# Moving half of one weight load to another queue, and cutting one VectorE task into six, in an attention and feed-forward kernel with a written-out order

## The chip, the cores and the metric

The kernel runs on one core of one Trainium2 chip. The core has a matrix engine (TensorE, PE in the profile; its weight loads are PEld), VectorE (DVE), ScalarE (ACT), GpSimd (POOL) and SyncE (SP), which issues most DMAs. Matmuls write to PSUM, eight banks of 128 partitions by 512 float32; all other data lie in SBUF. Each engine works through its own instruction stream in order and waits on semaphores for what other engines or DMAs have to deliver. The metric is the device time of one execution in microseconds (us), the median of several; lower is better.

## The reference

The input x has 2048 rows of 512 bfloat16 numbers. Three things are computed from it and mixed:

```python
g = sigmoid((x * gate_w).sum(-1, keepdims=True))     # one number per row
a = attention(x, wq, wk, wv, wo, beta)
b = ((relu(x @ W_gate) * (x @ W_up)) @ W_down)       # inner width 1792
out = g * a + (1 - g) * b
```

The attention has 32 heads of width 16. The rows are cut into 4 segments of 512. Inside a segment it is a causal softmax attention. Beside it each head keeps a memory, `M += phi(k).T @ v` and `z += sum(phi(k))` with `phi(t) = t + 1 if t > 0 else exp(t)`, from which the next segments read `phi(q) @ M / (phi(q) @ z)`. A gate per head, `sigmoid(beta)`, weighs memory against softmax. The head gates, called so below, are these 32 numbers and one minus them, spread over the partitions in the layouts that later steps want.

## The kernel before

All weights are loaded once and stay in SBUF. The work goes by segment (four) and inside a segment by column chunk c of 128, which holds 8 heads. For each segment x is wanted transposed (`xT`) and, for the row gate, untransposed (`xn`). `proj_q`, `proj_k` and `proj_v` are matmuls with the weights, each followed by a copy out of PSUM (VectorE, or ScalarE for half of v). For k, three masked copies into `KT` (L569) follow the copy. Scores come in fills of four PSUM banks (L617, and L630 for the diagonal blocks); ScalarE takes their exp (L639), GpSimd masks them (L668), and TensorE multiplies them with v (L690). `memory` (L801) forms M and z. `ffn_tasks` (L845) forms relu(gate) on ScalarE (L854) and its product with up on VectorE (`hT`, L860). `out_tile` (L871) adds the down projection and the attention's output projection in one PSUM bank.

Nearly every step of this is a task: `plan.add(engine, duration, key, emit, deps, ...)`. Durations, latencies and the table `LANDS` (when each first load is thought to be in) are numbers of a planner that ran beforehand. It is not in the file; its results are: `ORDER` lists all tasks by number in the order in which they are emitted, and `UNITS` gives for each buffer that a task needs (a PSUM bank, a ring buffer) which one it gets. Each engine executes its tasks in the order of that list. So the durations in the file have no effect on the chip; the order does.

What comes ahead of the list, in the order of the program: the loads (L300 to L328), each on the queue of the engine that issues it. SyncE (`nc.sync`) issues nearly all; ScalarE (`nc.scalar`) issues half of segment 0's `xn` and one quarter of `wq`. Segment 0's x comes in two halves: columns 0 to 255 as rows in `xn`, which TensorE transposes by a matmul with the identity (L500), and columns 256 to 511 by a DMA transpose (L304). So q of segment 0 is formed in two halves (L540 to L545): the first half of its four matmuls per chunk needs the first half of wq and `xn`, the second half needs wq's second half (L306) and the DMA transpose.

Two more pieces matter. `heat` (L901) is a warm-up: seven matmuls on constants in front of everything. `head_gates` (L385) is one VectorE task of 25 small instructions; it waits for `eb` (L398, ScalarE's exp of beta), which waits for the load of `betab` (L312). The row gate's dot product with `gate_w` is L417, one VectorE task per 128 rows; it reads `xn`, which is loaded anew for each segment (L276).

Of the kernel before, what the change touches and what calls it, by code (L numbers as in the profile page):

```python
# [178 lines left out]
def kernel(  # L179
# [205 lines left out]
    def head_gates():  # L385
# [4 lines left out]
        for m in range(4):  # L390
            rows = slice(32 * m, 32 * m + 32)
            nc.vector.tensor_copy(gcat[rows, 1], g[rows, 1, :, m])  # L392
            for c in range(NC):
                nc.vector.tensor_copy(gcat[rows, 0, c], g[rows, 0, c, (m + c) % 4])  # L394
# [11 lines left out]
    def K(unit, part=0.0):  # L406
        return unit * UNIT + part
# [563 lines left out]
```

## Time and profile before

| | us |
|---|---|
| median of 3 runs | 264.85 (264.78 to 265.1) |
| the profiled execution's own time | 264.56 |
| its span in the profile | 262.6 |
| TensorE busy | 258.0 (98%) |
| VectorE busy | 203.6 (78%) |
| ScalarE busy | 183.2 (70%) |
| GpSimd busy | 63.2 (24%) |

The span is the time from the first to the last instruction of the core; the rest of the execution's time lies around it. A matmul's row in the profile lasts longer than the distance to the next one, as matmuls overlap, so waits of TensorE are best read from the distances between starts. In a timeline line the columns are start, length, engine, line, operation, what is written and read, the shape and how many; in brackets stands how long the engine was idle before it and what it waited for. In the lines of waits the figures are the total in us, how often, and the longest.

### The profile page before, as it was taken

What the parts mean: (1) busy time and instruction counts of PE and PEld (TensorE: products, weight loads), DVE (VectorE), ACT (ScalarE), POOL (GpSimd) and SP (SyncE); (2) the same over time, 40 slices, a digit from 0 to 9 for tenths busy, and PEclk for the clock granted to TensorE, in tenths of its full rate; (3) what the DMA queues carried; (4) which work ended last, traced back from release to release, by engine and by line L of the source; (5) the groups of instructions that cost most, each with busy time, mean ns of one, the idle gap of its engine ahead of it and who ended that gap; (6) DMA issues with size and microseconds to landing.
All of it is one profiled execution on the core that took longest, in us unless ns stands there. A gap on an engine that the chain in (4) does not pass through costs nothing.

```text
span 262.6 us, 8919 instructions
## 1 busy us (share of the span) xinstructions
PE 258.0 (98%) x3867; PEld 117.4 (45%) x3867; DVE 203.6 (78%) x472; ACT 183.2 (70%) x168; POOL 63.2 (24%) x168
## 2 busy tenths in 40 slices
PE   8999999999999999999999999999999999999995
PEld 3434434454444354544444444444445444445454
DVE  2799999999895756959998977584998786768622
ACT  3299889999788688888586767788575767883000
POOL 8024353212321323232111321122121242121000
PEclk9999999999999999999999999999999999999999
DMA  7999974020402122100211112002110101120011
GB/s 193 301 264 308 312 148 122 4 42 12 94 3 74 46 67 67 49 2 2 81 21 25 54 31 103 22 12 82 35 47 6 54 2 62 70 76 19 2 42 42
DMA packets 31566, 19.72 MB, mean 75 GB/s; under 512 B 16040, under 2 KB 29992, under 8 KB 31528
## 3 DMA queue, kind: packets, MB, share of 16 engines
q1 hardware_dynamic: 31112, 18.90, 26.0%
q8 instruction: 30, 0.49, 0.8%
q10 hardware_dynamic: 416, 0.26, 0.3%
q14 instruction: 8, 0.07, 0.1%
HBM read 13.21 MB, written 2.55 MB: 60 GB/s over the span
## 4 chain that ended last, share of the span: by engine, by line
PE 91%; DMA 3%; SPq 2%; DVE 2%; issue 0%; ACT 0%
PE ps L463 52%; PE ps L467 21%; PE ps L617 8%; PE ps L690 7%; DMA betab<-in_A_beta_dram 3%; SPq L266 2%; PE ps L630 1%; PE ps L810 1%; DVE gcat L394 1%; SPq L304 1%; PE ps L746 0%; PE ps L786 0%; SPq L310 0%; DVE gcat L392 0%; DVE hT L860 0%
## 5 line engine op out<-in xcount | busy, mean ns | idle before, releaser
L639 ACT ACTIVATE E<-ps 128x2048 bf16<-128x2048 f32 x64 | 120.1, 1876 | 30.0 <-PE ps L617 20.1
L668 POOL TENSOR_SCALAR_AFFINE_SELECT E<-E 128x256 bf16<-128x256 bf16 x128 | 54.6, 451 | 172.9 <-ACT E L639 172.8
L860 DVE TENSOR_TENSOR hT<-ps,rgr 128x512 bf16<-128x512 f32 x56 | 38.0, 685 | 20.3 <-PE ps L463 11.8
L463 PE MATMUL ps<-xT,wu_sb 128*128 128x512 bf16 x172 | 47.1, 380 | 0.0
L854 ACT ACTIVATE rgr<-ps 128x512 bf16<-128x512 f32 x56 | 32.7, 596 | 16.9 <-PE ps L463 10.3
L463 PE MATMUL ps<-xT,wg_sb 128*128 128x512 bf16 x152 | 41.9, 380 | 0.5 <-DVE hT L860 0.5
L463 PE MATMUL ps<-wd_sb,hT 128*128 128x512 bf16 (+1 forms) x165 | 38.3, 353 | 0.0
L721 DVE STREAM_TRANSPOSE T<-ps 128x512 f32<-128x512 f32 x32 | 22.4, 706 | 7.5 <-PE ps L690 7.2
L617 PE MATMUL ps<-QT,KT 32*128 32x320 bf16 (+3 forms) x512 | 25.4, 273 | 0.0
L463 PEld LDWEIGHTS <-wu_sb 128*128 128x128 bf16 x172 | 15.6, 98 | 19.3 <-issue 2.5
L463 PEld LDWEIGHTS <-wg_sb 128*128 128x128 bf16 x152 | 14.1, 98 | 18.1 <-issue 2.5
L886 DVE TENSOR_SCALAR osr<-ps,ngcol 128x512 bf16<-128x512 f32 (+2 forms) x18 | 12.4, 689 | 11.8 <-PE ps L467 8.0
L463 PEld LDWEIGHTS <-hT 128*128 128x128 bf16 x165 | 14.2, 98 | 16.1 <-issue 2.5
L467 PE MATMUL ps<-wd_sb,hT 128*32 128x512 bf16 (+1 forms) x348 | 21.3, 362 | 0.0
L467 PE MATMUL ps<-xT,wg_sb 128*32 128x512 bf16 x288 | 19.8, 379 | 0.0
L617 PEld LDWEIGHTS <-KT 32*128 32x128 bf16 x512 | 7.6, 92 | 26.4 <-issue 25.4
L690 PE MATMUL ps<-E,Vp 128*17 128x320 bf16 (+3 forms) x512 | 19.3, 273 | 0.0
L639 ACT ACTIVATE Em<-ps 128x2048 bf16<-128x2048 f32 x8 | 15.0, 1873 | 3.1 <-PE ps L630 3.1
L463 PE MATMUL ps<-wv_sb,xT 128*128 128x512 bf16 x60 | 16.4, 380 | 0.0
L463 PE MATMUL ps<-xT,wq_sb 128*128 128x512 bf16 x54 | 15.4, 385 | 0.3 <-DMA wq_sb<-in_A_wq_dram 0.3
L467 PE MATMUL ps<-xT,wu_sb 128*32 128x512 bf16 x208 | 14.9, 379 | 0.0
L463 PE MATMUL ps<-xT,wk_sb 128*128 128x512 bf16 x54 | 14.6, 380 | 0.0
(102 smaller groups left out, 299.7 us busy)
## 6 DMA issues: line engine op xcount, KB each, us to landing
out_dram<-osr SPq DMA_DIRECT2D x15, 128.0 KB
wd_sb<-in_B_W_down_dram SPq DMA_DIRECT2D x2, 896.0 KB
xn<-in_A_x_dram SPq DMA_DIRECT2D x3, 512.0 KB
cdr<-coefs SPq DMA_DIRECT2D x6, 256.0 KB
xn<-coefs SPq DMA_DIRECT2D x6, 256.0 KB
wg_sb<-in_B_W_gate_dram SPq DMA_DIRECT2D x2, 512.0 KB
wu_sb<-in_B_W_up_dram SPq DMA_DIRECT2D x2, 512.0 KB
wg_sb<-in_B_W_gate_dram SPq DMA_DIRECT2D x2, 384.0 KB
```

The costliest lines, as they stand in the source:

```text
L266: eng.dma_start(out=dst, in_=src)
L304: nc.sync.dma_start_transpose(out=xT[0][:, NC // 2:NC, :], in_=x[0:L, halves[1]])
L463: nc.tensor.matmul(out, lhsT=lhsT, rhs=rhs, start=start, stop=stop)
L467: nc.tensor.matmul(out[r], lhsT=lhsT[:, r], rhs=rhs, start=start, stop=stop, tile_position=(0, 32 * j))
L617: nc.tensor.matmul(ps[:, j * L + o:j * L + o + L - q], lhsT=KT[i][rows, kb, 3 * r:3 * r + 2].rearrange("p h q -> p (h q)"), rhs=QT[i][rows ...
L639: last_exp[0] = [plan.add("ACT", 66 + 4 * L / 1.2, key, lambda: nc.scalar.activation(dst, ps[:, 0:4 * L], ACT.Exp, scale=SCALE), [a] + war ...
L668: nc.gpsimd.affine_select(out=m[:, :, o:o + HP], in_=m[:, :, o:o + HP], compare_op=ALU.is_ge, fill=0.0, base=HP, pattern=[[0, 4], [1, HP]] ...
L690: nc.tensor.matmul(bank(sl)[32 * m:32 * m + HW, q:q + w], lhsT=(Vp[i] if n < 4 else Vm)[:, kb, r, 4 * c + j, 0:HW], rhs=rhs, start=(n == 0 ...
L721: done.append(plan.add("DVE", 633, key - RL, lambda r=r, sl=sl: nc.vector.transpose(T[ts.i][:, r], bank(sl)), [a] + done, 75 if r else 0, ...
L854: r = plan.add("ACT", 478, key - RL, lambda sl=gsl, rs=rs: nc.scalar.activation(rgr[rs.i][:], bank(sl), ACT.Relu), [g], ACL, frees=[gsl])
L860: nc.vector.tensor_tensor(hT[hs1.i][:], bank(sl), rgr[rs.i][:], ALU.mult)),
L886: nc.vector.tensor_scalar(osr[os.i][:, n0 - c0:n1 - c0], bank(sl)[:, 0:n1 - n0], ngcol[:, tt:tt + 1], None, ALU.mult)),
```

## The change

It has four parts, and a new `ORDER` and `UNITS` that go with them.

- wq's second half is loaded from ScalarE's queue instead of SyncE's. It is issued as ScalarE's third DMA, right behind its share of the first half, while SyncE issues the DMA transpose of x.
- The task `head_gates` becomes six tasks: the three instructions that form the gates, four times `row_gates(m)` (five copies each), and `pair_gates` (two instructions). Their durations add up to 3240 ns in place of 2000. The instructions are the same 25.
- The last matmul of the warm-up has 128 columns instead of 384.
- Planner's numbers: several landing times in `LANDS`, the latency of the later loads of `xn` (7500 for 6500), and a dependency that fixes the order of the four transposes of segment 0's x.

```diff
-    LANDS = dict(n0=3700, n1=3750, q0=4750, q1=4750, x0=6500, qb=6700, ka=7900, kb=9300,
+    LANDS = dict(n0=3470, n1=3600, q0=4650, q1=4650, x0=6300, qb=6000, ka=7900, kb=9300,
...
-    got_q.append(load_rows(nc.sync, wq_sb, A_wq, 1, "q"))
+    got_q.append(load_rows(nc.scalar, wq_sb, A_wq, 1, "q"))
...
         nc.vector.tensor_tensor(gall[:, 0], eb[:], gall[:, 1], ALU.mult)
+
+    def row_gates(m):
         g = gall.rearrange("p k (c j r) -> p k c j r", j=4, r=2)
-        for m in range(4):
-            rows = slice(32 * m, 32 * m + 32)
-            nc.vector.tensor_copy(gcat[rows, 1], g[rows, 1, :, m])
-            for c in range(NC):
-                nc.vector.tensor_copy(gcat[rows, 0, c], g[rows, 0, c, (m + c) % 4])
+        rows = slice(32 * m, 32 * m + 32)
+        nc.vector.tensor_copy(gcat[rows, 1], g[rows, 1, :, m])
+        for c in range(NC):
+            nc.vector.tensor_copy(gcat[rows, 0, c], g[rows, 0, c, (m + c) % 4])
+
+    def pair_gates():
         for r, m in enumerate((mcol_e, mcol_o)):
             nc.vector.tensor_scalar(bdg[:, :, r], gcat[:, 1, :, r], m[:, 0:1], None, ALU.mult)
...
-    got_gates = plan.add("DVE", 2000, 0.0, head_gates, [got_eb], 100, lock=True)
+    got_gates = plan.add("DVE", 700, 0.0, head_gates, [got_eb], 100, lock=True)
+    got_gates = [plan.add("DVE", 560, 0.0, lambda m=m: row_gates(m), [got_gates], 100, lock=True)
+                 for m in range(4)]
+    got_gates = plan.add("DVE", 300, 0.0, pair_gates, got_gates, 100, lock=True)
...
                 a = plan.add("PE", 214, K(-9 + ci) + t, flip, [got_n[0][t]], PEL, need=[sl], size=4)
+                if prev:
+                    a.deps.append((prev, 0.0))
+                prev = a
...
-            w = L if k < 6 else 3 * P
+            w = L if k < 6 else P
...
-    plan.add("PE", 3680, -1e9, heat, lat=0, need=warm, frees=warm, size=14)
+    plan.add("PE", 3470, -1e9, heat, lat=0, need=warm, frees=warm, size=14)
...
-                                   6500, xfer=1700.0)]
+                                   7500, xfer=1700.0)]
```

The lists `ORDER` and `UNITS` are replaced as a whole; five more tasks shift the numbers of all that follow. Read engine by engine, this is what differs in the first 45 us:

- TensorE, behind the transposes: before, six first-half matmuls of q, then a second half, with the last two first-half matmuls between the second halves, and chunk 1's second half behind all of k. After: all eight first halves, the four second halves, then k of chunk 0, then the rest of k and the first score. From there on both orders have the same steps between two scores, in another sequence.
- VectorE, before: copies of q of chunks 3, 2 and 0, copy and masks of k of chunk 0, and so on; after v of tile 0 the whole of the head gates, then hT of feed-forward block fv0. After: copies of all four q, then k; behind v of tile 0 the first gate task and one row task, hT of fv0, v of tile 2, one L417, a row task, one L417, the phi of k, hT of fv1. The last two row and pair tasks come 30 to 35 tasks later, and 35 tasks behind segment 0's first L417 stands the first L417 of segment 1 (before, it stood after the second chunk's work on q and k).
- SyncE, first DMAs of the list: before, x's transpose for segment 2 (L273), pK of chunks 1, 0 and 2 (L582), then `xn` for segment 1 (L276). After: pK of chunk 0, `xn` for segment 1, x's transpose for segment 2, pK of chunks 2 and 1.
- GpSimd: three of the four gate spreads (L433) come ahead of the mask of chunk 1's first fill instead of behind it.

Later on the largest move is that of segment 2's `memory` step, about 35 us ahead on TensorE.

More of the change, by code (lines that the diff above doesn't have):

```diff
@@ L30 @@
 ORDER = """
[62 rows of a table removed]
[62 rows of a table added]
 """
 UNITS = (
-    "456701237654304000311112222211121102100000310000000230110000021000100002301130311100323232"
-    "34200321252207303631280009301d223a012b022c001112000100031030201012122131231200301104560132"
-    "000003200000002201100000210001000030011302201202231003a32231237103431062118022b20353209112"
-    "d201c0211100131320132000020011232301322322031456701230000023000000031011000000100020000120"
-    "11123270201023211a20172131312b30240238321600391005112d320c10020112223201123030223131033001"
-    "3456201300000030000000230110000002000000072011323330222130213110243007122a31082016320b3125"
-    "4139022d105c11000210011"
+    "456701237654310000231213121203110023000000210000000310110000001000100002301130210110222232"
+    "04301331053227100601183039303d120a312b223c001112003230031020230102221001012122101114563021"
+    "000003200000002201100000310001000002011302221202231210a10231007323431253218203b32060029123"
+    "d313c1102110032320020410232301120101322323031456710230000023000000032011000000200000000030"
+    "1101300021211a31221238320311373225001630041129012b213d320c00121201222211023230202136272001"
+    "1256210300000320000000330110000011000000075011312202201031020a2224303821033105322630071139"
+    "002d713c124b11000210011"
 )
@@ L492, in x0_tasks @@
     def x0_tasks():
-        got = []
+        got, prev = [], None
         for ci in range(NC // 2):
```

124 rows, old and new, of the table ORDER are left out of this document.

## The prediction

> **What bounds the kernel now.** I read the page's busy times first, then who waited for whom on TensorE, then its timeline in the first 25 us, then the rows of the engines that end those waits. The page's first part:
>
> ```profile
> PE 258.0 (98%) x3867; PEld 117.4 (45%) x3867; DVE 203.6 (78%) x472; ACT 183.2 (70%) x168; POOL 63.2 (24%) x168
> ```
>
> TensorE is busy for all but 4.6 us, of which 0.84 lie before its first matmul and 2.9 behind its last. A change that removes no matmul can win only TensorE's own waits. These are all of them, in the whole run:
>
> ```profile
> PE ps L905 <- PEq L955: 0.8, 1, 0.8
> PE ps L463 <- DVE hT L860: 0.5, 1, 0.5
> PE ps L463 <- DMA wq_sb<-in_A_wq_dram: 0.3, 1, 0.3
> ```
>
> The rows of a matmul overlap (a row lasts 0.38), so these figures are short by the overlap. The pace is what counts: twelve matmuls take 2.70 in the chain and eleven 2.48, so one costs 0.216. TensorE's timeline where the two waits lie:
>
> ```profile
> 4.77 1.69 PE L463 MATMUL ps<-xT,wq_sb 128*128 128x512 bf16 x6
> 6.75 1.90 PE L463 MATMUL ps<-xT,wq_sb 128*128 128x512 bf16 x8 [0.29 <-DMA wq_sb<-in_A_wq_dram]
> ...
> 11.60 0.40 PE L617 MATMUL ps<-QT,KT 32*128 32x448 bf16 x8
> ...
> 17.65 0.40 PE L617 MATMUL ps<-QT,KT 32*128 32x320 bf16 x8
> ...
> 18.43 0.59 PE L463 MATMUL ps<-xT,wg_sb 128*128 128x512 bf16 x2
> 19.56 1.89 PE L463 MATMUL ps<-xT,wg_sb 128*128 128x512 bf16 x8 [0.54 <-DVE hT L860]
> 21.38 0.40 PE L617 MATMUL ps<-QT,KT 32*128 32x320 bf16 x8
> ...
> 24.41 0.41 PE L630 MATMUL ps<-QT,KT 32*128 32x64 bf16 x32
> ```
>
> The first six end at 6.46, so the last began at 6.08 and the next could begin at 6.29; it began at 6.75: **wait A, 0.46**. Likewise 18.43 + 0.59 - 0.38 + 0.22 = 18.86 against 19.56: **wait B, 0.70**. Scores (L617, L630) come every 3.03, and at 17.65 to 21.38 after 3.73, which is 3.03 plus wait B. After 19.56 TensorE waits for nothing until its last matmul. VectorE's timeline shows what holds wait B, and SyncE's a load that the change moves:
>
> ```profile
> 7.39 1.99 DVE L550 CAST QT<-ps 128x512 bf16<-128x512 f32 x3 [2.40 <-PE ps L463]
> 10.05 0.69 DVE L566 CAST ktr<-ps 128x512 bf16<-128x512 f32 x1 [0.68 <-PE ps L463]
> ...
> 15.62 0.18 DVE L386 TENSOR_SCALAR gall<-eb 128x32 f32<-128x32 f32 x1 [0.18 <-ACT eb L398]
> ...
> 16.33 0.15 DVE L392 COPY gcat<-gall 32x8 f32<-32x8 f32 x1
> ...
> 16.83 0.16 DVE L392 COPY gcat<-gall 32x8 f32<-32x8 f32 x1
> ...
> 18.83 0.68 DVE L860 TENSOR_TENSOR hT<-ps,rgr 128x512 bf16<-128x512 f32 x1
> ```
> ```profile
> 32.95 1.73 SPq L273 DMA_TRANSPOSE xT<-in_A_x_dram  x1
> 34.80 3.82 SPq L582 DMA_TRANSPOSE pK<-pkT  x3
> 38.72 0.52 SPq L276 DMA_DIRECT2D xn<-in_A_x_dram  x1
> ```
>
> The head gates hold VectorE from 15.62 to 18.83, 3.21 in one piece. Behind them stands hT, which frees the PSUM bank that the 19.56 matmul needs.
>
> **The change, part by part.** *Warm-up.* Its seventh matmul loses 256 of 384 columns. The warm-up runs at 0.43 per 512 columns (its weight loads begin at 2.50 and 2.93), so it ends 0.21 sooner, at 3.46 instead of 3.68. The first transposes' weights load at 3.46, when xn lands, and take 0.10, so they start at 3.56: 0.12 won. Little of it lasts: the pace turns fast at 5.25 in the trace's clock record, and until then a matmul costs 0.43. The first wq matmul starts at 4.66 instead of 4.77, but the third at 5.38 instead of 5.43. I count 0.05.
>
> *wq's second half on ScalarE's queue.* It takes 0.57 of issue from SyncE and puts about 0.5 on ScalarE, ahead of its table load (1.87, 1.28 long). That then ends near 3.65, while ScalarE's first copy is wanted at 4.2: hidden, with 0.55 to spare. In the trace's semaphore records the transposed half of x lands at 5.75 and wq's second half at 6.70. Now they share the 16 engines, whose share is 0.97 and 1.05 at 5 to 7 us. x lands between 5.75 (sharing costs nothing) and 6.70 (both end when the second ends now); I take 6.5, since the engines are full. The Trainium skill ("DMA: Bandwidth & Descriptors", Issuing engines are not separate DMA queues) speaks against any gain: all queues run on the same 16 engines and a second issuer saves issue time alone. By that rule x lands at 6.70 and the sum below loses 0.08; the trace's full engines agree.
>
> *The order in front of the first score.* The new order runs all eight first-half matmuls of q before any second half; the old one kept two of them behind the waiting one. Eight from 4.66 fill TensorE until 6.67, so wait A goes. What is late next is VectorE: four q casts (0.65 each, from 1.99 for three) now stand ahead of k's first cast, instead of three and a pause of 0.68. The first cast starts 0.64 behind its matmul (6.75 to 7.39): 6.67 + 0.64 + 4 x 0.65 = 9.91. From that cast to the score it takes 11.60 - 10.05 = 1.55: 11.46. TensorE itself gets there at 6.67 + 20 x 0.216 + 0.1 = 11.09, so it waits 0.37 in a new place. Gain at the first score: 0.14, not 0.46. If x lands at 6.70 it is 0.06. The weights wk land at 7.50 and 8.33 and are wanted at 8.2 and 8.6.
>
> *Head gates as six tasks.* The 25 instructions stay the same and cost the same 3.2. The new order puts the first task (15.62 to 16.33, 0.71) and one row task (0.50) ahead of hT, and the other four later. The start does not move: ScalarE's eb waits for betab until 15.36. hT's matmuls end at about 16.9 and hT itself at 17.6; TensorE wants the bank at 11.46 + 6.06 + 0.33 = 17.85. Wait B goes, with 0.2 to spare: the fourth score comes at 11.46 + 9.09 = 20.55, 0.83 ahead of 21.38.
>
> *What is late then.* VectorE reaches the first row dot of x (L417) at 18.2, but the xn rows land at 19.0: it idles 0.8. From 19.03 the next hT (fv1) comes after two dots (0.7 each), a gate row (0.5), a phi (0.66) and itself (0.6), at 22.3, and a matmul wants it at 22.1: 0.2 lost. ScalarE went on from 15.36 without a pause as before; its fourth exp ends near 23.65 and allows the fifth score at 23.7. So that comes at 23.8 against 24.41: **0.6 won**.
>
> *The loads moved on SyncE.* The new order moves the load of xn for the second segment (L276) ahead of x's transpose (L273) and of two of the three pK transposes. The row dot that reads it, on VectorE at 43.03 now, is placed about 35 tasks behind 19.03, which sum to 17.6: 36.7 at the earliest, some 37.5 with its waits on TensorE. SyncE cannot start the moved list before 32.95 (its first DMA waits for wd); one pK transpose takes 1.2, so the load is issued at 34.2. The three such loads land 4.0, 3.5 and 5.4 after issue: 38.2, 37.7 or 39.6. VectorE stands until then, and behind the dot are an hT and a V cast: 0.62 + 0.20 + 0.61 + 0.69 + 0.26 + 0.61, with 0.1 to the bank's release. TensorE wants that bank near 41.1, so the dot must start by 38.0. I take 38.1 (0.1 lost), with 0 and 1.6 as ends. x's transpose and the other pK transposes go later by about a microsecond each, but are wanted at 53 and beyond 64. POOL's gate spreads pass in front of a mask, under POOL's 172.9 us of idle time. The segment-2 memory matmul moves 35 us ahead; its pK transpose has about 10 us, and such a one lands 2.1 to 2.4 after issue. The planner's switches between tile shapes are 151 in both orders, and no matmul is added.
>
> Sum: 0.14 (start) + 0.70 (wait B) - 0.2 (hT) - 0.1 (xn) = 0.5. The profiled execution has 264.56, with 262.6 of span and 2.0 around it, 0.29 under the median of 264.85; it would be 264.05. Against the median: **264.35**.
>
> **Rivals.** *More is won:* xn lands by 37.7 and the bank for fv1 comes in time. For it: both misses are 0.1 to 0.2. Against: VectorE is 94% busy from 19.56 to 60 us. Gain 0.14 + 0.70 = 0.85: 264.0.
>
> *The moved load decides, and the kernel is slower.* If xn needs the 5.4 us of the third such load, VectorE stands until 39.6 and TensorE loses 39.6 - 38.0 = 1.6: 264.85 - 0.6 + 1.6 = 265.85. It turns the sign from a landing at 38.6. For it: the old order read that load only 0.3 after it landed (42.71, read at 43.03), and the new one reads it 3.9 after its issue instead of 4.3. Against: two of three loads make it by 38.2.
>
> *The change of queue does nothing or harm:* the transpose of x suffers beside wq and lands at 7.2. Then the first score comes at 7.25 + 0.64 + 2.6 + 1.55 = 12.0, 0.4 late, which eats most of wait B: 264.75.
>
> *The clock.* TensorE pauses 0.1 between the warm-up and the transposes, which it doesn't now. If that starts the count anew, the fast pace comes 4.4 (0.84 to 5.25) after 3.56, near 7.95; the eight matmuls end at 8.0, the first score is at 12.8, the fourth at 21.9: 0.5 late, 265.35. The Trainium skill ("TensorE: Matmul & The Clock Gate", Part 1) has such a window, 3.4 us of sustained activity that runs free; by that rule a pause of 0.1 matters little, and no run here shows one.
>
> **How the numbers follow.** Forecast 0.47 (264.0 to 264.7), more won 0.19, late xn 0.20 (265.2 to 266.2), late x 0.09, clock 0.05. A measurement of this kernel tells about 0.2%, 0.53 us, from no change. Faster (under 264.32): 0.26 of the forecast and 0.19: 0.45. Same: 0.21 + 0.04 + 0.07 + 0.01 = 0.33. Slower (over 265.38): 0.16 + 0.02 + 0.04 = 0.22. The range 263.8 to 265.5 leaves out the lowest 0.04 and 0.14 of the late loads and the clock.
>
> **What would show it.** Right: no wait of TensorE on wq near 6.7, a wait on KT of about 0.4 before the first score at 11.4 to 11.5, hT for fv0 near 17, the fourth score near 20.5, the fifth near 23.8, and VectorE idle before L417 at 19. Wrong: an idle VectorE before L417 at 37 to 39 with a wait of TensorE behind it, matmuls at 0.43 beyond 5.3, or any wait of TensorE after 45, where I costed the reshuffled order at nothing because the old one has none and VectorE's idle time grows from 60 us on.

## The result and the profile after

In the first comparison the changed kernel took 263.94 us (263.61 to 264.48, seven runs) and the kernel before 265.1 (264.78 to 265.99, seven runs): ratio 0.995, 95% interval 0.9935 to 0.9965, so 0.9 to 1.7 us faster. The forecast was 264.35 against 264.85, a gain of 0.5. Three copies of the changed kernel, run later beside the kernel before, gave 264.19 against 264.79 (0.9973, 0.9962 to 0.9983), 264.09 against 264.72 (0.9969, 0.9953 to 0.9985) and 264.03 against 264.64 (0.9971, 0.9958 to 0.9984). By these the gain is 0.6 us between the medians and 0.4 to 1.2 by the intervals. The first comparison's 1.16 is nearly twice that, and more than half of the difference is in its kernel before, whose 265.1 is 0.3 to 0.5 above its medians in those three. In the last of the three one execution of the kernel before took 907.52 us and is left out of the ratio.

The profiled execution took 264.48, the slowest of its seven, with a span of 262.7. Its busy times:

```profile
PE 257.8 (98%) x3828; PEld 117.4 (45%) x3828; DVE 204.9 (78%) x472; ACT 183.7 (70%) x168; POOL 64.2 (24%) x168
```

All waits of TensorE in that execution:

```profile
PE ps L469 <- DMA xT<-in_A_x_dram: 1.0, 1, 1.0
PE ps L914 <- PEq L964: 0.8, 1, 0.8
```

Before there were two besides the start: one on wq (wait A) and one on hT (wait B). Wait B is gone. In wait A's place stands a longer one, and it is for the DMA transpose of x. TensorE's timeline:

```profile
4.75 2.01 PE L469 MATMUL ps<-xT,wq_sb 128*128 128x512 bf16 x8
7.73 1.89 PE L469 MATMUL ps<-xT,wq_sb 128*128 128x512 bf16 x8 [0.97 <-DMA xT<-in_A_x_dram]
9.45 2.75 PE L469 MATMUL ps<-xT,wk_sb 128*128 128x512 bf16 x12
12.34 0.40 PE L626 MATMUL ps<-QT,KT 32*128 32x448 bf16 x8
...
18.40 0.40 PE L626 MATMUL ps<-QT,KT 32*128 32x320 bf16 x8
18.73 2.33 PE L469 MATMUL ps<-xT,wg_sb 128*128 128x512 bf16 x10
...
21.42 0.40 PE L626 MATMUL ps<-QT,KT 32*128 32x320 bf16 x8
...
24.45 0.41 PE L639 MATMUL ps<-QT,KT 32*128 32x64 bf16 x32
```

The eight first-half matmuls run in one go, as foreseen, and then nothing happens for 0.97. The first score comes at 12.34, where it was 11.60: 0.74 late. From the third score to the fourth it takes 3.02, where it was 3.73. So at the fourth score this execution is level with the one before (21.42 against 21.38), and it stays there: over the later scores the difference is 0.04 to 0.09, but for one score at 66 us and for the stretch from 128 to 228 us, where the new order places some scores elsewhere; the last two are 0.08 late. VectorE's timeline shows the new place of the gates:

```profile
8.36 2.48 DVE L559 CAST QT<-ps 128x512 bf16<-128x512 f32 x4 [3.40 <-PE ps L469]
10.76 0.68 DVE L575 CAST ktr<-ps 128x512 bf16<-128x512 f32 x1
...
16.49 0.16 DVE L386 TENSOR_SCALAR gall<-eb 128x32 f32<-128x32 f32 x1
...
17.30 0.17 DVE L393 COPY gcat<-gall 32x8 f32<-32x8 f32 x1
17.38 0.37 DVE L395 COPY gcat<-gall 32x2 f32<-32x2 f32 x4
17.79 0.69 DVE L869 TENSOR_TENSOR hT<-ps,rgr 128x512 bf16<-128x512 f32 x1
18.39 0.68 DVE L605 CAST Vp<-ps 128x512 bf16<-128x512 f32 x1
18.99 0.68 DVE L423 SCALAR_TENSOR_TENSOR junk<-xn,gwb 128x512 bf16<-128x512 bf16 x1
```

Ahead of hT stand only the first gate task and one row task, 1.30 from their start to that of hT (16.49 to 17.79) in place of 3.21.

**One number tells the rest.** The first score's start and the time of the same execution, for the two traces of the kernel before and the four of the changed one (landings from the trace's semaphore records; "offset" is the time less the first score):

| kernel | x's transpose lands | wq's second half lands | first score | time | offset |
|---|---|---|---|---|---|
| before | 5.75 | 6.70 | 11.60 | 264.56 | 252.96 |
| before, again | 6.40 | 7.17 | 12.07 | 264.95 | 252.88 |
| changed | 7.69 | 6.78 | 12.34 | 264.48 | 252.14 |
| changed, again | 7.45 | 6.50 | 12.11 | 264.26 | 252.15 |
| changed, third | 7.49 | 6.51 | 12.15 | 264.66 | 252.51 |
| changed, fourth | 6.74 | 5.95 | 11.40 | 263.55 | 252.15 |

The change takes 0.73 to 0.81 off the offset, in three of its four traces. Wait B, of 0.70 and 0.52 in the two traces of before, makes up most of it, and the start then decides, with one more place that the third copy shows.

The rest of the offset lies outside the span. Time less span is 1.94 and 2.03 in the two traces of before, and 1.70 to 1.80 in the four of the changed kernel. The other runs agree: on average over a kernel's runs it is 1.88 to 1.92 for the kernel before and its variants, and 1.70 to 1.75 for every variant with the new order, whatever its queue, gates and warm-up. So 0.16 to 0.20 of the 0.6 is won outside the span, and it goes with the new order; what makes it no trace shows.

### The profile page after: what moved, and what is told of

Read it like the earlier page. It is cut to its first block, busy times and chain, and to the rows that moved or that the text cites. A ratio compares the mean times of both kernels' runs of the same rounds, so it can differ in the third digit from the quotient of the medians.

```text
span 262.7 us, 8841 instructions
## 1 busy us (share of the span) xinstructions
PE 257.8 (98%) x3828; PEld 117.4 (45%) x3828; DVE 204.9 (78%) x472; ACT 183.7 (70%) x168; POOL 64.2 (24%) x168
## 4 chain that ended last, share of the span: by engine, by line
PE 94%; DMA 2%; DVE 2%; SPq 0%; issue 0%
PE ps L469 56%; PE ps L473 20%; PE ps L626 8%; PE ps L699 7%; DMA xT<-in_A_x_dram 2%; PE ps L639 1%; DVE QT L559 1%; PE ps L819 1%; PE ps L795 0%; PE ps L755 0%; SPq L266 0%; DVE KT L578 0%; DVE ktr L575 0%; DVE osr L895 0%
## 5 line engine op out<-in xcount | busy, mean ns | idle before, releaser
L469 PE MATMUL ps<-xT,wu_sb 128*128 128x512 bf16 x168 | 45.9, 380 | 0.0
L469 PE MATMUL ps<-wd_sb,hT 128*128 128x512 bf16 (+1 forms) x174 | 40.3, 354 | 0.0
L469 PEld LDWEIGHTS <-hT 128*128 128x128 bf16 x174 | 15.2, 98 | 17.1 <-issue 2.1
L473 PE MATMUL ps<-xT,wg_sb 128*32 128x512 bf16 x280 | 18.6, 379 | 0.0
L473 PE MATMUL ps<-wd_sb,hT 128*32 128x512 bf16 (+1 forms) x312 | 17.8, 360 | 0.0
L469 PE MATMUL ps<-xT,wq_sb 128*128 128x512 bf16 x60 | 16.4, 382 | 1.0 <-DMA xT<-in_A_x_dram 1.0
L559 DVE CAST QT<-ps 128x512 bf16<-128x512 f32 x16 | 10.7, 687 | 6.4 <-PE ps L469 6.2
```

The source lines that it names most:

```text
L469: nc.tensor.matmul(out, lhsT=lhsT, rhs=rhs, start=start, stop=stop)
L473: nc.tensor.matmul(out[r], lhsT=lhsT[:, r], rhs=rhs, start=start, stop=stop, tile_position=(0, 32 * j))
L559: prj["q", seg, c] = plan.add("DVE", 600, key - RQK, lambda: nc.vector.tensor_copy(QT[i][:], bank(sl)), [a], DVL, frees=[sl])
```

## The experiments

All kernels compute the whole reference. Four sets were run; those of one set share a chip and the runs of the kernel before.

### The changed kernel again, and its parts alone

**The changed kernel, unaltered.**

> The changed kernel once more. Mixing theory (x's DMA transpose is slowed by the plain load of wq that runs beside it on ScalarE's queue): x lands between 7.2 and 7.8 again, TensorE waits 0.7 to 1.1 for xT near 7, first score at 12.0 to 12.4, fourth at 21.1 to 21.5. Chance theory (7.69 was one execution's bad luck): x lands anywhere from 5.8 up, and the first score moves with it. Both: 0.9 to 1.3 us under the kernel before, as measured, and the same distance between the fourth score and the end.

Measured 264.19 (263.78 to 264.38), ratio 0.9973 (0.9962 to 0.9983). Against the first trace of the changed kernel every one of the 72 scores comes 0.23 sooner, and x's transpose lands 0.24 sooner (7.45 against 7.69): the whole difference is in the start. The 0.9 to 1.3 under the kernel before that were expected did not come again; it was 0.6.

**The changed kernel with the queue put back.**

```diff
-    got_q.append(load_rows(nc.scalar, wq_sb, A_wq, 1, "q"))
+    got_q.append(load_rows(nc.sync, wq_sb, A_wq, 1, "q"))
```

> The changed kernel with wq's second half back on SyncE's queue, behind the transpose; order, gates and warm-up as changed. Mixing theory: x lands at 5.7 to 5.9 as before the change, wq at 6.7, TensorE waits under 0.15 near 6.7, first score at 11.4 to 11.6 (VectorE's four copies set it, 0.3 to 0.4 of TensorE waiting for KT), fourth at 20.5 to 20.7; the time is 0.5 to 0.9 us under that of the changed kernel. Chance theory: same time as the changed kernel within 0.2, and x's landing as scattered.

Measured 264.27 (263.78 to 265.82), ratio 0.9982 (0.9967 to 0.9997); x landed at 6.42 and wq's half at 7.17, the first score came at 11.85. x is earlier than in the changed kernel, though not as early as expected, but the gain of 0.5 to 0.9 on the changed kernel did not come.

**The kernel before with only the queue changed.**

```diff
-    got_q.append(load_rows(nc.sync, wq_sb, A_wq, 1, "q"))
+    got_q.append(load_rows(nc.scalar, wq_sb, A_wq, 1, "q"))
```

> The kernel before with only the queue of wq's second half changed. Mixing theory: x lands at 7.2 to 7.8, first score at 12.2 to 12.6; the wait behind the head gates shrinks by as much, so from the fourth score on it is only 0.2 to 0.4 late: 0.2 to 0.4 us slower than before. Chance theory: within 0.2 of before, x near 5.8.

Measured 265.04 (264.61 to 265.51), ratio 1.0003 (0.9991 to 1.0015); x at 7.28, wq's half at 6.34, first score 12.16. In either order the queue alone is worth nothing that can be told, and x's landing is later with it in each trace. The two rows below are the mean rate of the DMA engines from 5.00 to 6.00 (the last two columns are their busy share and GB/s), first of the kernel before, then of the changed one:

```profile
5.00:5.50 0.50, 0.50 (x3) 0.21 (x2) 0.00 (x0) 0.14 (x1) 0.37 (x2) 1.00 0.90 218
5.50:6.00 0.50, 0.50 (x4) 0.22 (x3) 0.00 (x0) 0.00 (x0) 0.44 (x5) 1.00 1.03 322
```
```profile
5.00:5.50 0.50, 0.50 (x3) 0.20 (x2) 0.00 (x0) 0.12 (x1) 0.37 (x2) 1.00 1.33 110
5.50:6.00 0.50, 0.50 (x4) 0.24 (x3) 0.00 (x0) 0.00 (x0) 0.44 (x5) 1.00 0.25 54
```

In the changed kernel's trace the transpose's packets and those of the plain load on the other queue are under way together, and 110 and 54 GB/s get through where the kernel before moves 218 and 322. x lands 1.94 later there, although in the kernel before wq's half lands only 0.95 behind x (5.75 to 6.70). But a slow stretch is no mark of the mixture. These are the same rates in the trace of the changed kernel with the queue put back, where wq's half comes behind the transpose:

```profile
4.00:4.50 0.50, 0.50 (x8) 0.50 (x6) 0.40 (x1) 0.18 (x1) 0.50 (x4) 1.00 1.44 125
4.50:5.00 0.50, 0.42 (x3) 0.04 (x1) 0.45 (x2) 0.45 (x2) 0.48 (x4) 1.00 0.86 69
```

From 4.15 to 5.00 only packets of SyncE's queue start there, all of them under 512 bytes, as the transpose's are, at 85 GB/s. So the transpose can be about as slow with no data of a plain load beside it. That a load beside it delays x is read from the landings, further down; why the slow stretch comes, and why it is longer in some executions, stays open.

**The kernel before with only the gates cut in six,** the pieces placed as far behind one another as in the new order.

```diff
-        order = [self.tasks[int(n)] for n in ORDER.split()]
+        ids = [n + 5 * (n > 26) for n in map(int, ORDER.split())]
+        for n, behind in ((30, 26), (27, 45), (29, 43), (28, 246), (31, 99)):
+            ids.insert(ids.index(behind) + 1, n)
+        order = [self.tasks[n] for n in ids]
...
-    got_gates = plan.add("DVE", 2000, 0.0, head_gates, [got_eb], 100, lock=True)
+    got_gates = plan.add("DVE", 700, 0.0, head_gates, [got_eb], 100, lock=True)
+    got_gates = [plan.add("DVE", 560, 0.0, lambda m=m: row_gates(m), [got_gates], 100, lock=True)
+                 for m in range(4)]
+    got_gates = plan.add("DVE", 300, 0.0, pair_gates, got_gates, 100, lock=True)
```

> The kernel before with the head gates cut into six tasks (first task and one row task in the old place, the others put behind later VectorE tasks), nothing else. Both theories: the wait of 0.70 before the 19.56 matmul goes to under 0.1, the fourth score comes at 20.6 to 20.8, and the time falls by 0.5 to 0.7. If the gain of the change came from the reshuffled order instead, the time stays within 0.2.

Measured 264.88 (264.75 to 265.27), ratio 1.0003 (0.9993 to 1.0013): no gain. Yet wait B is gone: from 21 to 36 us every score comes 0.66 sooner than in the kernel before, at 39.4 it is only 0.29 sooner, and from 42.4 to the end 0.11 later. What takes it back are two waits of TensorE, here with VectorE's lines ahead of them:

```profile
34.46 0.68 DVE L869 TENSOR_TENSOR hT<-ps,rgr 128x512 bf16<-128x512 f32 x1
35.16 0.16 DVE L396 COPY gcat<-gall 32x8 f32<-32x8 f32 x1
35.24 0.80 DVE L398 COPY gcat<-gall 32x2 f32<-32x2 f32 x4
36.08 0.69 DVE L575 CAST ktr<-ps 128x512 bf16<-128x512 f32 x1
...
39.95 0.68 DVE L869 TENSOR_TENSOR hT<-ps,rgr 128x512 bf16<-128x512 f32 x1
```
```profile
36.83 0.59 PE L472 MATMUL ps<-xT,wq_sb 128*128 128x512 bf16 x2 [0.20 <-DVE ktr L575]
40.69 0.59 PE L472 MATMUL ps<-xT,wg_sb 128*128 128x512 bf16 x2 [0.24 <-DVE hT L869]
```

The k cast starts at 36.08 and that hT at 39.95; in the kernel before they started at 36.01 and 39.31. TensorE runs 0.66 ahead and wants them sooner, and the late gate pieces make them later.

### Does the cut or the order bring the gain?

**The changed kernel with its six gate tasks in one piece.**

```diff
-        order = [self.tasks[int(n)] for n in ORDER.split()]
+        ids = [int(n) for n in ORDER.split()]
+        for n in (30, 29, 28, 27):
+            ids.remove(n)
+            ids.insert(ids.index(26) + 1, n)
+        ids.remove(31)
+        ids.insert(ids.index(30) + 1, 31)
+        order = [self.tasks[n] for n in ids]
```

> The changed kernel with its six gate tasks put back in one piece behind eb; nothing else is moved. Theory (the cut removes the wait for hT fv0's bank): the gates hold VectorE about 3.2 us in one piece from 16.5, hT fv0 comes near 19.4 in place of 17.8, TensorE waits for it, and the fourth score comes 3.5 to 3.8 behind the third in place of 3.03. The 0.5 to 0.8 stay to the end, since TensorE has no other wait to give them back in: the ratio to the kernel before is 0.999 to 1.001. Rival (the new order alone is worth it, since the cut alone brought nothing): all scores stay 3.03 apart and the ratio is near 0.997, as with the six tasks apart.

Measured 265.79 (265.57 to 266.23) against 265.01, ratio 1.003 (1.0017 to 1.0043): the new order without the cut is slower than the old one. TensorE and the VectorE line that it waits for:

```profile
17.99 0.40 PE L632 MATMUL ps<-QT,KT 32*128 32x320 bf16 x8
20.12 2.32 PE L475 MATMUL ps<-xT,wg_sb 128*128 128x512 bf16 x10 [1.73 <-DVE hT L875]
```
```profile
19.38 0.68 DVE L875 TENSOR_TENSOR hT<-ps,rgr 128x512 bf16<-128x512 f32 x1
```

The wait is back and has grown to 1.78 (4.81 from the third score to the fourth, less 3.03), where 0.5 to 0.8 was expected. From the first score, hT is 0.21 later than in the kernel before (19.38 - 11.94 against 18.83 - 11.60), and TensorE wants its bank 0.9 sooner: right behind the third score, where the old order put four other matmuls in between. All later scores keep 1.37 to 1.38 against the changed kernel; nothing gives it back.

**The kernel before, gates cut, and two steps moved out of the way of the late pieces:** phi(k) with its transpose (0.76) and phi(q) (0.71) of segment 1's first head go behind the hT at 39.95.

```diff
+        for n in (361, 370, 369):
+            ids.remove(n)
+            ids.insert(ids.index(258) + 1, n)
```

> The kernel before with the gates cut in six, as in the run that won 0.66 at 21 us and lost it again at 36 to 42, and with two steps that are wanted late moved out of the way: the phi(k) of segment 1's first head with its transpose (0.76) and its phi(q) (0.71) go behind the hT at 39.95. Theory (the late gate pieces, 1.45 us at 35.2 to 37.1, pushed the k cast and that hT past what TensorE wants): the k cast and hT come 0.6 sooner, the 0.66 won at 21 us stays to the end, and the ratio is 0.997 to 0.998 in place of 1.000. Rival (VectorE is full up to 60 us, so whatever is moved is late elsewhere): the gain is lost at a later place and the ratio stays at 1.000.

Measured 264.8 (264.3 to 265.79) against 265.01, ratio 0.9998 (0.9982 to 1.0013). The k cast came at 35.41 and the hT at 38.50, and the 0.61 won at 21 us lasted one score longer, to 39.4. Then 0.50 went at once:

```profile
41.76 0.38 PE L475 MATMUL ps<-xT,wu_sb 128*128 128x512 bf16 x1 [0.34 <-DVE Vp L608]
```
```profile
40.43 0.70 DVE L714 STREAM_TRANSPOSE oT<-och 128x512 bf16<-128x512 bf16 x1
41.06 0.65 DVE L608 CAST Vp<-ps 128x512 bf16<-128x512 f32 x1
```

The moved steps now stand ahead of the V cast, which is late in their stead, and the rest went by 51 us. So the rival holds here: VectorE is nearly full in that stretch (busy for 9.29 of the 10 us from 33 to 43), and mending one lateness makes the next. The cut and the new order take 0.73 to 0.81 off the offset together; by itself the cut brought no gain in the places tried, and the new order without it was slower.

### The start: two DMAs at once

**ScalarE's load behind a small copy,** meant to start it behind the table load.

```diff
+    tiny = sb([P, 1], BF16, "tiny")
+    nc.scalar.copy(tiny[:], nc.const_aps.tensor(1.0, (P, 1), BF16))
     got_q.append(load_rows(nc.scalar, wq_sb, A_wq, 1, "q"))
```

> The changed kernel with a one-column copy on ScalarE ahead of its load of wq's second half, so that ScalarE loads its table first and issues that load at about 3.2 in place of 1.87, still on its own queue. Theory (a plain load that runs at the same time as the DMA transpose slows it): x's transposed half lands at 5.8 to 6.4 in place of 7.45 to 7.69, wq's half at 6.6 to 7.2, the first score comes at 11.4 to 11.9 in place of 12.1 to 12.3, and the 0.4 to 0.7 stay to the end: ratio 0.995 to 0.996. ScalarE's own start (its copy at 4.2) isn't touched. Rival (the queue as such, or two loads of the same bytes in any order): x lands at 7.3 or later again and the ratio is 0.997.

Measured 264.2 (263.32 to 265.0) against 265.01, ratio 0.9968 (0.9953 to 0.9983). The load was not delayed; ScalarE's queue in the trace:

```profile
1.87 1.28 ACT L307 ACT_TABLE_LOAD   x1 [1.87 <-issue]
1.93 0.40 ACTq L266 DMA_DIRECT2D wq_sb<-in_A_wq_dram  x1
3.16 0.19 ACT L307 COPY tiny<-const-bfloat16-1.0 128x1 bf16<-128x1 bf16 x1
```

The DMA is issued at 1.93 while the engine loads its table and before the copy that stands ahead of it. So this is one more execution of the same two loads side by side, and a lucky one: wq's half landed at 5.60, x at 6.54, the first score came at 11.20. It doesn't test the theory.

**ScalarE's load held back by a real dependence:** the copy writes into the place that the load fills.

```diff
+    nc.scalar.copy(wq_sb[:, 2, 0:1], nc.const_aps.tensor(1.0, (P, 1), BF16))
     got_q.append(load_rows(nc.scalar, wq_sb, A_wq, 1, "q"))
```

> The changed kernel with ScalarE's load of wq's second half made to wait for a one-column copy of ScalarE into the place that it fills, so that it really starts at 3.2 to 3.5 in place of 1.9, with its queue unchanged. Theory (the two loads slow each other when their packets run at the same time): x lands at 5.6 to 6.4, wq's half at 6.6 to 7.2, the first score comes 4.65 behind the later one, 11.3 to 11.9, and the ratio is 0.995 to 0.997. Rival (a load on the second queue takes turns whenever it starts, since x's packets are still to come at 3.5): x lands at 7.0 or later and the ratio is 0.997 to 0.998.

Measured 265.47 (264.63 to 267.28) against 264.72, ratio 1.0025 (1.0008 to 1.0042). The load was issued at 3.39. x landed at 6.24, early again as the theory said. But wq's half landed at 8.74, not 6.6 to 7.2: wk's first half, issued at 3.19 on SyncE, runs ahead of it and beside it (8.55). TensorE waits for the weights instead:

```profile
PE ps L470 <- DMA wq_sb<-in_A_wq_dram: 2.2, 1, 2.2
```

The half of the expectation that speaks of x holds, the ratio was wrong.

**A second load beside the transpose:** wk's first half on ScalarE's queue too.

```diff
-    got_k = [load_rows(nc.sync, wk_sb, A_wk, i, "k") for i in range(2)]
+    got_k = [load_rows(eng, wk_sb, A_wk, i, "k") for i, eng in enumerate((nc.scalar, nc.sync))]
```

> The changed kernel with a second load beside the transpose: wk's first half also goes by ScalarE's queue, at about 2.4. Theory (plain loads beside the DMA transpose take its turns on the 16 engines): x's transposed half lands 0.7 to 1.5 later once more, at 8.2 to 9.0, the first score comes near 12.8 to 13.6, and the ratio is 1.000 to 1.003. Rival (x was late in these executions for another reason): it lands at 7.4 to 7.7 as with one load beside it, and the ratio is 0.997. ScalarE's table load ends 0.5 later, at about 4.2, just when its first copy is wanted: at most 0.2 of the loss is from there.

Measured 268.31 (267.48 to 270.13) against 265.01, ratio 1.0136 (1.0106 to 1.0167). x landed at 9.29, later than the 8.2 to 9.0 expected, later than in any trace with one load beside it (6.54 to 8.12), and 1.6 later than in the first trace of the changed kernel. The first score came at 15.42, 3.08 later than there, and only 1.6 of that is the landing. The rest is the clock. Windows of the trace (the column ahead of the last two is the granted clock, the first figure behind the colon's pair the length, the next TensorE's busy time):

```profile
6.50:9.30 2.80, 0.00 (x0) 0.10 (x1) 0.00 (x0) 0.00 (x0) 0.01 (x1) 1.00 1.17 254
9.30:10.40 1.10, 1.07 (x5) 0.48 (x5) 0.44 (x1) 0.00 (x0) 0.00 (x0) 1.00 1.09 346
10.50:13.80 3.30, 3.30 (x10) 1.11 (x9) 2.26 (x5) 0.00 (x0) 0.00 (x0) 0.50 1.10 346
```

TensorE stood for 2.86, worked at full pace for a microsecond, and then had half the clock for 3.41 (10.46 to 13.87 in the clock record). The pause of 0.97 in the changed kernel brings no such stretch.

**Both loads on SyncE's queue, wq's half first.**

```diff
-    nc.sync.dma_start_transpose(out=xT[0][:, NC // 2:NC, :], in_=x[0:L, halves[1]])
-    got_x0b = arrival("x0")
-    got_q.append(load_rows(nc.scalar, wq_sb, A_wq, 1, "q"))
+    nc.sync.dma_start(out=wq_sb[:, 2:4, :],
+                      in_=A_wq.rearrange("(c p) n -> p c n", p=P)[:, 2:4, :])
+    nc.sync.dma_start_transpose(out=xT[0][:, NC // 2:NC, :], in_=x[0:L, halves[1]])
+    got_x0b = arrival("x0")
+    got_q.append(arrival("qb"))
```

> The changed kernel with both loads on SyncE's queue, wq's second half first and x's transpose behind it, so that ScalarE's queue has only the first loads of xn and wq and has emptied by 4.6, before the transpose's packets start. Theory (only a plain load on the other queue at the same time slows the transpose): wq's half lands near 5.3, x at 6.4 to 6.7, the first score comes at 11.0 to 11.4 and the time is 263.2 to 263.6: ratio 0.993 to 0.995, the best of all. Rival (the transpose's packets are slow beside any load, so wk behind it on the same queue does the same): x lands at 7.2 or later and the ratio is 0.997.

Measured 264.27 (262.99 to 264.51) against 264.72, ratio 0.9968 (0.9954 to 0.9982). In the trace x landed at 6.66, as the theory had it, wq's half at 5.65 and not near 5.3, and the first score came at 11.47, just past the range; but the offset is 252.51, and the median is no lower than that of the changed kernel. One of its runs took 262.99, the lowest of the study. What the trace shows to have gone wrong behind the first score is the subject of the next part; why the other executions were not faster at the start, no trace shows.

### The moved load of xn

**The changed kernel, a third time.**

> The changed kernel as it is, once more, so that the others of this chip stand beside it. Theory (behind the first score nothing waits, so the time is the first score plus 252.15, as in four traces of the new order: 252.14, 252.15, 252.16, 252.12): x's transposed half lands somewhere from 6.5 to 7.7, the first score comes 4.65 to 4.7 later, 11.2 to 12.4, and the time of the profiled run is that plus 252.1 to 252.2. Median 263.9 to 264.2, ratio 0.996 to 0.998. Rival (something behind the first score differs from run to run too): the offset falls outside 252.05 to 252.25.

Measured 264.09 (263.47 to 265.13) against 264.72, ratio 0.9969 (0.9953 to 0.9985). The offset, 252.51, is outside what the theory allowed, so the rival is right: something behind the first score differs too. Up to the tenth score this trace is 0.19 ahead of the first one of the changed kernel, from the eleventh on 0.25 behind: 0.44 is lost between them. VectorE's line there:

```profile
38.79 0.94 DVE L423 SCALAR_TENSOR_TENSOR junk<-xn,gwb 128x512 bf16<-128x512 bf16 x1 [0.51 <-DMA xn<-in_A_x_dram]
39.67 0.08 DVE L423 DVE_READ_ACCUMULATOR junk<-xn,gwb 128x1 f32 x1
39.67 0.38 DVE L740 TENSOR_TENSOR cfr<-cfr,grc 128x32 f32<-128x32 f32 x1
39.97 0.68 DVE L869 TENSOR_TENSOR hT<-ps,rgr 128x512 bf16<-128x512 f32 x1
```

This is the row dot that waits for the moved load. It was issued at 34.23 and landed at 38.77, 4.54 later; in the first trace it took 33.94 to 37.91, and the dot started at 38.40 without a wait.

**The longer warm-up again.**

```diff
-            w = L if k < 6 else P
+            w = L if k < 6 else 3 * P
```

> The changed kernel with the seventh warm-up matmul back at 384 columns. Theory (the warm-up's length shifts the first transposes by 0.12 and the first-half matmuls by 0.1, and TensorE then waits for x anyway): the first score is x's landing plus 4.65 as before, and the ratio is the changed kernel's own of this chip within 0.0005. Rival (a pause of 0.1 between the shorter warm-up and the transposes starts the clock's count anew, so the longer one brings the fast pace sooner): the fast pace comes at least 1 us sooner than in the changed kernel and the time falls by 0.3 or more.

Measured 264.2 (263.82 to 264.82), ratio 0.9968 (0.9952 to 0.9984), beside 0.9969 of the changed kernel in the same set. The warm-up's length is worth nothing that can be told. In its trace VectorE waits 0.45 for xn, and 0.13 is lost at the eleventh score.

**The changed kernel, a fourth time,** beside the two that follow.

> The changed kernel as it is, beside the next two on one chip. Theory (two places are left that differ from run to run: x's landing ahead of the first score, and the moved load of xn at 37.7 to 38.8, which cost 0.44 and 0.13 in two of the last four traces and nothing in four others): time is the first score plus 252.15 plus what VectorE waits for xn beyond 38.2; median 263.9 to 264.2, ratio 0.996 to 0.998.

Measured 264.03 (263.54 to 264.7) against 264.64, ratio 0.9971 (0.9958 to 0.9984); x at 6.74, first score 11.40, offset 252.15, no wait for xn.

**The load of xn one place further ahead,** before the pK transpose that stood in front of it.

```diff
+        ids = [int(n) for n in ORDER.split()]
+        ids.remove(343)
+        ids.insert(ids.index(66), 343)
+        order = [self.tasks[n] for n in ids]
```

> The changed kernel with the moved load of xn put one place further ahead, before the pK transpose that stands in front of it on SyncE's queue. Theory (that load is issued 1.35 us late behind the transpose, whose issue it waits for): it is issued near 32.6 in place of 33.5 to 34.2 and lands at 36.5 to 37.8, VectorE never waits for it, the eleventh score keeps its place behind the tenth in every run, and the median falls by 0.05 to 0.2 against the changed kernel. Rival (the load is late because the last weights still land until 34, whenever it is issued): it lands at 38 or later again and nothing changes.

Measured 264.16 (263.5 to 264.92), ratio 0.9976 (0.9963 to 0.9988). In the trace the load was issued at 33.23, as SyncE still waits there for earlier loads, and landed at 37.40, in time for a dot at 38.83 in an execution with a late start. The wait is gone in this trace and the offset is 252.14, but the median is no lower than that of the changed kernel (264.03). This execution shows how far the start can slip: x landed at 8.12, TensorE waited 1.9 for it, and its time was 264.92.

**Both mended:** wq's half and x in that order on SyncE, and xn early.

> Both loads of the first segment on SyncE's queue with wq's second half ahead of x's transpose, and the load of xn ahead of the pK transpose. Theory (x's landing and the moved load are the two places that take the gain back): x lands at 6.4 to 6.9, the first score comes at 11.2 to 11.6, no wait at the eleventh score, time 263.4 to 263.8: ratio 0.994 to 0.996, faster than the changed kernel by 0.3 to 0.6. Rival (the start is as late in most executions, and the one trace at 11.47 was a lucky one): the median stays at 264.1 to 264.3.

Measured 264.04 (263.64 to 264.38), ratio 0.997 (0.996 to 0.9981). Its trace is close to what the theory drew (x at 6.99 and the first score at 11.65, each a little past the range; no wait at the eleventh score; 263.70), and its runs lie closer together than those of the others. The median is still the changed kernel's. So no version of this study beats the change by an amount that can be told.

**The kernel before, a second trace.**

> The kernel before as it is, for a second trace of it. Theory (x's landing is early there, and the wait for hT fv0's bank, 0.70 in the first trace, is what it pays): x lands at 5.6 to 6.0, the first score comes at 11.5 to 11.8, the third to fourth take 3.6 to 3.75 in place of 3.03, and the time is the first score plus 252.7 to 253.1. Rival (the first trace's wait was one execution's): under 3.3 between the third and the fourth.

One time, 264.95. x landed at 6.40, wq's half at 7.17, the first score came at 12.07 (expected by 11.8), and from the third score to the fourth it took 3.55, so wait B was 0.52, a little under what was expected; offset 252.88. TensorE's line:

```profile
19.86 1.67 PE L463 MATMUL ps<-xT,wg_sb 128*128 128x512 bf16 x7 [0.37 <-DVE hT L860]
```

## Why the prediction was right or wrong, point by point

**Wait B: right.** Inside the span the term of 0.70 was the gain: 0.70 and 0.52 in two traces of before, nothing in twelve traces of the new order with six gate tasks, and 1.78 when the gates are put in one piece. What the prediction didn't see is that the cut needs the new order. It costed the reshuffle at nothing and the cut at 0.70; alone the cut won 0.66 and lost it by 42 us.

**The start: the step that failed.** x's landing was bounded by 5.75 and 6.70, "both end when the second ends now". With wq's half beside it from the first, it landed at 6.54 to 8.12 in nine traces (7.69, 7.45, 7.49, 6.74, 8.12, 7.46, 7.28, 7.28, 6.54), and at 5.64 to 6.42 in the five with that half behind it on SyncE. The bound supposed that two loads side by side end no later than one behind the other. In the two traces with wq's half ahead of x on SyncE's queue x landed at 6.66 and 6.99, so one behind the other the bound nearly holds; side by side seven of the nine are later than both, the middle one at 7.45. The term of the start was +0.14, and between the two profiled executions the first score came 0.74 later instead. What in the side-by-side transfer costs the time stays open, as the rates above show no difference of kind. The rival "x's transpose suffers beside wq", with 7.2 and a first score at 12.0, got a chance of 0.09 and is nearest to the landings. Its gain of 0.1 is that of the two profiled executions (0.08), though not that of the medians. The Trainium skill ("DMA: Bandwidth & Descriptors", Issuing engines are not separate DMA queues) says that DMAs of different queues interleave on the same engines and that a second issuer saves only issue time. The prediction took from it a landing at 6.70; eight of the nine traces are later, so here the second issuer cost more than that.

**The working from the landing to the first score: right.** 0.64 + 2.6 + 1.55 = 4.8 from the later landing was in the rival's sum; 4.65 to 4.68 was measured in eleven traces of the new order (4.81 in the one with wq's half and x in that order on SyncE and xn late, 6.13 in the one with the slow clock). In the old order it is 4.88 to 4.90 (11.60 - 6.70, 12.07 - 7.17, and three more). So at a landing of 6.70 the new order is worth 0.24, where the prediction had 0.06, and a landing at 7.45, the middle one of the nine, takes three times that back against wq's 6.70.

**Why the queue isn't a loss in the median then** is settled only in part. With wq's half on SyncE behind x, ScalarE's quarter of wq, issued at 1.31 in either case, landed at 4.61 to 5.32 in five traces; with it on ScalarE, at 4.34 to 4.53 in nine. That the transpose only meets another plain load then, and so costs as much elsewhere, would fit this, but is not shown. The experiments gave 1.0003 for the queue in the old order and 0.9973 against 0.9982 in the new.

**VectorE at 18 to 22 us: two small terms fell away.** VectorE was to stand 0.8 before the dot at 19.0 and to lose 0.2 at the next hT. The xn rows landed at 18.05 instead of 19.0, the dot started at 18.99 without a pause, and nothing was lost. The 19.0 was one execution's: the second trace of before has 18.28.

**The moved load of xn: right in place, and right within its ends.** Issue forecast 34.2, landing 37.7 to 39.6, loss 0.1 with 0 and 1.6 as ends. In the four copies of the changed kernel it was issued at 33.1 to 34.2, landed at 37.1 to 38.8 and cost 0, 0, 0.44 and 0; in three variants 0.06, 0.13 and 0.44. The rival that it decides, with 1.6, didn't come.

**The clock rival: not seen, though one run shows a slow clock behind a longer pause.** In the changed kernel's trace the fast pace came at 5.02, not near 7.95. Neither the warm-up's length nor pauses of 0.97, 1.9 and 2.2 slowed the clock; after one of 2.86 it was slow for 3.41 us, in one trace. The Trainium skill ("TensorE: Matmul & The Clock Gate", Part 1) speaks of a window of 3413 ns that runs free; the clock record of that trace agrees in its lengths (6.83 fast, 3.41 slow), and it shows that a pause of 2.86, shorter than the window, was enough there.

**After 45 us: right.** The new order has no wait of TensorE on another engine or a DMA there in any of its traces.

**The sum: near the mark by luck.** 0.14 + 0.70 - 0.2 - 0.1 was 0.5. Three comparisons measured 0.6; the first measured 1.16, more than twice the forecast. The terms that were off:

- The start was to win 0.14. The first score of the four copies came from 0.06 sooner to 0.88 later than the 11.46 put in.
- The 0.2 at hT's bank was not lost, nor, in three of the four copies, the 0.1 of xn.
- The time around the span was kept at 2.0 without a reason. It fell by 0.16 to 0.20.

The first is a loss that the sum lacks, the others are gains that it lacks, and they offset each other. The first comparison's 263.94 is nearly the 264.0 of the rival "more is won". In the profiled execution xn and the bank for fv1 cost nothing, as that rival has it, but its gain at the start did not come, so that number is luck too. The rest of the 1.16 isn't explained by any trace: the two profiled executions are only 0.08 apart (264.56 and 264.48), the kernel before has a spread of 264.2 to 266.2 in the later sets, the one long execution apart, its seven runs lay at 264.78 and above, and a landing that slips by a microsecond, as x's did, moves a whole execution by as much.

## What to carry to other kernels

Where TensorE is never idle behind its first dependent matmul, one start time and one constant describe an execution: read the first score, compare it score by score with another trace, and each step in that difference is a place that won or lost. A gap that is closed early is a gain only if every engine that feeds the bottleneck can keep up with the earlier pace; if it has no idle time ahead, the gain is handed back a few steps later, so cut and order have to be tried together. When a transfer is moved beside another one, don't bound its landing by their sum alone: beside one plain load this transpose landed anywhere from 6.54 to 8.12.

## What was not expected of the hardware

- The DMA transpose of x had stretches of half a microsecond at 54 to 125 GB/s, with a plain load beside it and without. With wq's half beside it x landed at 6.54 to 8.12, with that half behind it on the same queue at 5.64 to 6.42.
- A DMA on ScalarE's queue was issued while the engine was still loading its table, and ahead of a copy that stands before it in the kernel (1.93 against 3.16). A copy into the DMA's own destination held it back (issue at 3.39).
- TensorE's clock fell to half for 3.41 us after a pause of 2.86, and only a microsecond after work had been taken up again; after pauses of 0.97, 1.9 and 2.2 it did not.
- The time around the span, 1.88 to 1.92 us in the old order, was 1.70 to 1.75 in the new one.
